# Zeros products for TensorE in the first tile of an RWKV-6 + GELU-MLP kernel: 24 instead of 8 in front, and four 64x64 products instead of two 128x128 ones behind each burst

## The chip, the cores and the metric

The kernel runs on one core of one Trainium2 chip. The metric is the device time of one execution in microseconds. All numbers are microseconds unless marked otherwise.

## What is computed

```python
# r, k, v, w: (4, 8, 768, 48); u: (8, 48)
for t in range(S):
    cur = einsum('bhd,bhe->bhde', u * k[t], v[t])
    y[t] = einsum('bhd,bhde->bhe', r[t], state + cur)
    state = w[t] * state + k[t] (outer) v[t]
x = y as (3072, 384)
h = x @ w_in                     # (3072, 2048)
out = (0.5 * h * (1 + erf(h / sqrt(2)))) @ w_out   # (3072, 384)
```

## The kernel before

The 768 time steps of four batches are cut into eight tiles of T = 384 steps; a tile holds all eight heads, and is cut into chunks of C = 64. For each tile, `attention(x, unit)` makes y (transposed, `xT`) and `mlp(x)` makes the output rows. Attention inside a chunk goes over levels h = 1, 2, 4, 8, 16, 32: on each level PE multiplies the chunk's k against its r in bursts of small products (`products`, L452), an elementwise update on VectorE (L494, L505) folds the decay w into r and k in place, and a masked copy (L465, L516 on VectorE, L513 on ScalarE) takes the level's part of the burst out of PSUM into `a_sb`. A burst of a level needs the update of the level before, and an update needs the burst of its own level to be through.

The first tile (x = 0) is done as two units of two head pairs each, so that work starts when half of the data is there. The two units alternate: a burst of one, a burst of the other. Each burst of the first tile has 24 fp32 products of 64x64 on the four 64x64 quadrants of the array; the profile lists 48, as each is two passes. The quadrant is set by the partitions of the operands and of the output: `half = [slice(0, 64), slice(64, 128)]`, rows by `g`, columns by `p`; `g` also picks one of the two PSUM banks of a `pair`. There are three such pairs (`pd`), so a burst may also have to wait for a copy to empty a pair.

The first level has two bursts a unit, the level's own and a diagonal one (`diagonal`, with r*u from ScalarE, L401). After the levels come the transposes of k (`kt_ps`, L685), the products of k and v (`kv_ps`, L711), those of `a_sb` and v (`y_ps`, L752), the chain of states on VectorE (L731, L726), the products of r and the states (L797), and copies and three plus three small DMAs into `xT`. Then the first burst of tile 1 (again L452), six products of zeros (`warm`, L225) and the first product of the MLP (`h_ps`, L1059) follow on PE. From then on PE is given a mix of MLP products and small attention bursts of the next tile.

`keep_warm(n)` issues n bf16 products of zeros, 128x128 by 128x512, into a bank of the tag "mm" that nothing reads. It is called with 8 ahead of everything, with 2 behind the bursts of the first tile (12 times: all but the first burst of each unit's first level), and twice with 3 (other banks) before the MLP starts.

The order of the work on each engine is written out by hand: `PLAN[x]` is a string in which each letter takes one step of a stream ("." the first unit or the MLP, "s" the second unit or the tile's attention, "l" loads, "c" weight conversion), and each engine executes its instructions in that order. All loads are issued by SyncE's queue, some only after a small memset on VectorE (L163, L204) has set a buffer free. The first tile's loads are, in order, w of both units, then r and k of the first unit and r and k of the second (L150).

Of the kernel before, what the change touches and what calls it, by code (L numbers as in the profile page):

```python
# [10 lines left out]
F32 = mybir.dt.float32  # L11
# [21 lines left out]
BANK = 512  # L33
# [40 lines left out]
def kernel(  # L74
# [9 lines left out]
    nc = tc.nc  # L84
# [16 lines left out]
    ps = ctx.enter_context(tc.tile_pool(name="ps", bufs=1, space=PSUM))  # L101
# [4 lines left out]
    def pair(name):  # L106
        return pools["d"].tile([128, 2, BANK], F32, name=name, tag="d")
# [16 lines left out]
    half = [slice(0, 64), slice(64, 128)]  # L124
# [8 lines left out]
    bufs = [io.tile([128, 3 * NP * T], F32, name=f"rkw{i}", bufs=1) for i in range(2)]  # L133
# [78 lines left out]
    zeros = const.tile([128, BANK], BF16, name="zeros")  # L212
# [6 lines left out]
    def keep_warm(n, elsewhere=False):  # L219
        if elsewhere:  # L220
            t = pair("warm")[:, 0]
        else:
            t = ps.tile([128, BANK], F32, name="warm", tag="mm", bufs=2)
        for _ in range(n):
            nc.tensor.matmul(t, lhsT=zeros[:, 0:128], rhs=zeros, start=True, stop=True)  # L225

    keep_warm(8)


    masks = {h: const.tile([128, C // 2], U8, name=f"mask{h}") for h in LEVELS if h < 16}  # L230
# [122 lines left out]
    def attention(x, unit):  # L353
# [91 lines left out]
        def products(bs, right, width, rest=False):  # L445
            d = pair("d")
            n = 0
            for b in bs:
                for i in range(NI):
                    for g in range(2):  # L450
                        for p in range(2):
                            nc.tensor.matmul(d[half[p], g, n * width:(n + 1) * width],  # L452
                                             lhsT=kc[half[g], b, i, p], rhs=right(half[g], b, i, p),
                                             start=True, stop=True)
                    n += 1
            if x == 0 and not rest:
                keep_warm(2)
            return d[:, :, 0:n * width]

        def diagonal():  # L460
            return [products([b], lambda z, b, i, p: rucs[b][z, i, p], C) for b in range(np_)]
# [7 lines left out]
        def halves():  # L469

            for h in LEVELS:
                m = C // 2 // h
                if np_ < NPART:

                    d = products(range(np_), lambda z, b, i, p: rc[z, b, i, p], C, h == 1)
                    d = d.rearrange("p g (n m two j) -> p g n m two j", two=2, j=h, m=m)[:, :, :, :, 1, :]
                else:
                    right = rc.rearrange("p b i c (m two j) -> p b i c m two j", two=2, j=h)[:, :, :, :, :, 1, :]
                    d = products(range(np_), lambda z, b, i, p: right[z, b, i, p], C // 2)
                    d = d.rearrange("p g (n m j) -> p g n m j", j=h, m=m)  # L480
# [220 lines left out]
        def vs(b, i, g):  # L701
            o = ((parts[b] * NI + i) * 2 + g) * D
            return loaded[x][1][:, o:o + G]

        kvs = []
        for b in range(np_):
            kv_ps = pair("kv_ps")
            for i in range(NI):
                for p in range(2):
                    for g in range(2):  # L710
                        nc.tensor.matmul(kv_ps[half[g], p, i * D:(i + 1) * D], lhsT=k_t(b, i, p, g),  # L711
                                         rhs=vs(b, i, g)[half[p], 0:D], start=True, stop=True)
# [74 lines left out]
        for i in range(NI):  # L787
            for p in range(2):
                for b in range(np_):
                    q, c3 = divmod(i, N3)  # L790
                    for g in range(2):
                        c = 2 * c3 + (p + g) % 2
                        src, c0 = (st, c - 1) if c else (before, NC - 1)
                        if src is None:
# [3 lines left out]
                                         lhsT=src[half[g], o:o + G], rhs=rc[half[g], b, i, c % 2],  # L798
                                         start=False, stop=True, skip_group_check=True)
# [518 lines left out]
```

## Time and profile before

| | us |
|---|---|
| timed runs | 588.53, 588.55, 589.37 (median 588.55) |
| profiled execution, device time | 589.61 |
| its span, first to last instruction | 587.8 |
| PE busy / weight loads busy | 571.1 / 521.4 |
| VectorE / ScalarE / GpSimd busy | 425.5 / 291.2 / 58.6 |
| mean granted TensorE clock | 0.997 |
| front: first zeros product; eight of them | 2.29; 3.59 |
| first real product (L452) | 9.43 |
| first transpose (L685) | 31.97 |
| first product of the MLP (L1059) | 44.40 |

The profile is of one execution. A line of it names the engine, the line of the kernel, the operation and the tiles, output before input; the bracket behind tells how long the engine stood idle before and what ended that. "issue" means that the profile shows nothing that the engine waited for. PE's products overlap, and their ends are modelled, so starts are the safer numbers.

### The profile page before, as it was taken

The page shows a single profiled execution, that of the slowest core. Times are in us where ns is not written, and L with a number is a line of the kernel's source. Part 1 is how long each engine was busy: PE and PEld are TensorE (multiplying, and loading weights), DVE is VectorE, ACT ScalarE, POOL GpSimd, SP SyncE. Part 2 cuts the span into 40 slices and gives each one's busy share as a digit, 9 for nine tenths or more (in the row PEclk, how much of TensorE's full clock was granted, in tenths as well). Part 3 has the DMA queues.
Part 4 walks back from the last instruction along what each step waited for, and adds up shares of the span by engine and source line. Part 5 has one row for each costly group of instructions (what it writes and reads, how often), then busy time and mean ns, then how long its engine had stood idle before and what let it go on. Part 6 is the DMA issues. An engine that isn't in the chain of part 4 may idle for free. (4 is left out here: it accounts for less than half of the span.)

```text
span 587.8 us, 17656 instructions
## 1 busy us (share of the span) xinstructions
PE 571.1 (97%) x7602; PEld 521.4 (89%) x7616; DVE 425.5 (72%) x825; ACT 291.2 (50%) x668; POOL 58.6 (10%) x63
## 2 busy tenths in 40 slices
PE   5789999999999999999999999999999999999997
PEld 3576666799999999999999999999998999999997
DVE  5988968989758975777959986777759987420332
ACT  2368898446362567235462467245561467335400
POOL 3100000013000130012000130002100111003100
PEclk8999999999999999999999999999999999999999
DMA  6749742253032542354122632344224333114201
GB/s 230 221 135 352 265 168 78 79 142 52 5 89 64 157 58 41 90 142 93 26 55 79 151 70 44 86 139 74 27 41 119 86 42 42 29 45 55 28 13 35
DMA packets 62430, 55.09 MB, mean 94 GB/s; under 512 B 32400, under 2 KB 47504, under 8 KB 62352
## 3 DMA queue, kind: packets, MB, share of 16 engines
q1 hardware_dynamic: 50832, 45.62, 25.5%
q0 software_dynamic: 11424, 8.26, 10.8%
q8 instruction: 60, 0.98, 0.7%
q14 instruction: 18, 0.15, 0.1%
q10 hardware_dynamic: 96, 0.07, 0.1%
HBM read 36.24 MB, written 4.72 MB: 70 GB/s over the span
## 5 line engine op out<-in xcount | busy, mean ns | idle before, releaser
L929 PE MATMUL h_ps<-xT,w_in_sb 128*128 128x192 f32 x560 | 111.5, 330 | 0.6 <-DVE o_sb L1196 0.6
L980 POOL DMA_DIRECT2D g<-o_sb x42 | 50.6, 1229 | 478.2 <-ACT o_sb L965 468.9
L929 PEld LDWEIGHTS h_ps<-xT,w_in_sb 128*128 128x128 f32 x560 | 93.0, 190 | 4.7 <-ACT g L961 1.6
L929 PE MATMUL u_ps<-s,w_in_sb 128*128 128x192 f32 x224 | 41.2, 327 | 0.0
L1073 PE MATMUL o_ps<-w_out_sb,g 128*128 128x192 f32 x224 | 39.8, 326 | 0.0
L929 PEld LDWEIGHTS u_ps<-s,w_in_sb 128*128 128x128 f32 x224 | 37.1, 190 | 0.2
L1073 PEld LDWEIGHTS o_ps<-w_out_sb,g 128*128 128x128 f32 x224 | 37.0, 190 | 0.0
L604 ACT COPY a_sb<-d 32x256 f32<-32x256 f32 (+8 forms) x90 | 32.6, 362 | 4.9 <-PE d L588 3.4
L1059 PE MATMUL h_ps<-xT,w_in_sb 128*128 128x384 f32 x96 | 33.2, 494 | 0.0
L452 PEld LDWEIGHTS d<-rkw 64*64 64x64 f32 x1152 | 19.4, 138 | 14.7 <-issue 10.5
L1073 PE MATMUL o_ps<-w_out_sb,f 128*128 128x192 f32 x176 | 32.0, 331 | 0.0
L1073 PE MATMUL o_ps<-t,g 128*128 128x192 f32 x176 | 31.4, 330 | 0.0
L1073 PE MATMUL o_ps<-t,s 128*128 128x192 f32 x176 | 31.2, 328 | 0.0
L1073 PE MATMUL o_ps<-t,e 128*128 128x192 f32 x176 | 30.6, 326 | 0.5 <-issue 0.5
L621 DVE COPY_PREDICATED a_sb<-quarter,d 128x480 f32<-128x480 uint8 (+5 forms) x54 | 23.2, 439 | 10.5 <-PE d L588 9.3
L726 DVE SCALAR_TENSOR_TENSOR st<-st,tot_sb,kv_ps 128x48 f32<-128x48 f32 x160 | 28.9, 258 | 2.6 <-PE kv_ps L711 2.5
L1073 PE MATMUL o_ps<-w_out_sb,e 128*128 128x192 f32 x176 | 30.7, 328 | 0.0
L982 DVE TENSOR_TENSOR g<-g,o_sb 128x384 f32<-128x384 f32 x14 | 7.6, 549 | 31.2 <-ACT o_sb L965 31.1
L1073 PEld LDWEIGHTS o_ps<-t,e 128*128 128x128 f32 x176 | 28.9, 190 | 0.7 <-issue 0.7
L1073 PEld LDWEIGHTS o_ps<-t,g 128*128 128x128 f32 x176 | 28.6, 190 | 0.5
L1073 PEld LDWEIGHTS o_ps<-w_out_sb,f 128*128 128x128 f32 x176 | 28.5, 190 | 0.6
L1073 PEld LDWEIGHTS o_ps<-t,s 128*128 128x128 f32 x176 | 28.8, 190 | 0.2
(163 smaller groups left out, 1171.3 us busy)
## 6 DMA issues: line engine op xcount, KB each, us to landing
rkw<-in_rkw_dram SPq DMA_DIRECT2D x54, 256.0 KB, 3.6
g<-o_sb POOLq DMA_DIRECT2D x42, 192.0 KB, 3.6
raw<-in_w_out_dram SPq DMA_DIRECT2D x8, 768.0 KB, 6.2
v_in<-in_v_dram SPq DMA_DIRECT2D x8, 584.0 KB, 4.6
raw<-in_w_in_dram SPq DMA_DIRECT2D x5, 768.0 KB, 7.5
out_dram<-o_sb SPq DMA_DIRECT2D x20, 192.0 KB, 2.0
rkw<-kx SPq DMA_DIRECT2D x72, 48.0 KB, 2.0
rkw<-in_rkw_dram SPq DMA_DIRECT2D x6, 384.0 KB, 6.2
```

The costliest lines, as they stand in the source:

```text
L452: nc.tensor.matmul(d[half[p], g, n * width:(n + 1) * width], lhsT=kc[half[g], b, i, p], rhs=right(half[g], b, i, p), start=True, stop=True)
L604: nc.scalar.copy(out=at[z, g, first:behind, (a + 1) * h:], in_=d[z, :, :, to] if g == slice(None) else d[z, :, to])
L621: nc.vector.copy_predicated(out=an[:, :, :, :, (a + 1) * h:], mask=mask.to_broadcast(data.shape), data=data)
L726: nc.vector.scalar_tensor_tensor(out=stq[:, q, c], in0=stq[:, q, c - 1] if c else b4[:, q, NC - 1], scalar=totq[:, q, c:c + 1], in1=kvs[q ...
L929: nc.tensor.matmul(o, lhsT=lhsT, rhs=rhs, start=start, stop=True, skip_group_check=True)
L980: nc.gpsimd.dma_start(out=g, in_=z, accum_op=ALU.add)
L982: nc.vector.tensor_add(g, g, z)
L1059: nc.tensor.matmul(h_ps, lhsT=w_in_sb[:, f // FI, j, f % FI * 128:(f % FI + 1) * 128], rhs=xT[:, j, :], start=(j == 0), stop=(j == NJ - 1))
L1073: nc.tensor.matmul(o, lhsT=lhs(j), rhs=rhs(j), start=start and j == 0, stop=(j == HF - 1), skip_group_check=True)
```

## The change

The front gets 24 products of zeros in place of 8. Behind the bursts of the first tile, `keep_warm(2)` is replaced by `keep_warm_tiles()`: four bf16 products of zeros of 64 rows, 64 columns and 512 elements, one on each quadrant of the array, the two row halves into the two banks of the tag "mm". The six zeros products before the MLP stay as they are. PE's instruction stream gets 32 more instructions in front (16 weight loads and 16 products) and 8 in place of 4 at each of the 12 fillers.

```diff
         for _ in range(n):
             nc.tensor.matmul(t, lhsT=zeros[:, 0:128], rhs=zeros, start=True, stop=True)
 
-    keep_warm(8)
+    def keep_warm_tiles():
+
+        ts = [ps.tile([128, BANK], F32, name="warm", tag="mm", bufs=2) for _ in range(2)]
+        for p in range(2):
+            for g in range(2):
+                nc.tensor.matmul(ts[g][half[p]], lhsT=zeros[half[g], 0:64], rhs=zeros[half[g]], start=True, stop=True)
+
+    keep_warm(24)
...
             if x == 0 and not rest:
-                keep_warm(2)
+                keep_warm_tiles()
             return d[:, :, 0:n * width]
```

## The prediction

> **What bounds the kernel now.** I read the page first, then the first 45 us by themselves, because both edits lie there. The page gives the balance and where PE's program comes from:
>
> ```profile
> PE 571.1 (97%) x7602; PEld 521.4 (89%) x7616; DVE 425.5 (72%) x825; ACT 291.2 (50%) x668; POOL 58.6 (10%) x63
> ...
> PEclk8999999999999999999999999999999999999999
> ...
> q8 instruction: 60, 0.98, 0.7%
> ```
>
> PE is the bound of the run: the trace's records show no PE gap over 0.1 us between 40.04 and 190 us, and only five, 1.7 us together, from there to the end. So whatever brings the first L1059 product (44.40) forward reaches the end, if nothing later takes it back. Queue q8 brought 60 blocks (0.98 MB) for 7616 weight loads, 7602 products and some 150 waits: 256 PE instructions a block. That matters below.
>
> The windows show the clock at the start:
>
> ```profile
> 9.00:10.00 1.00, 0.57 (x21) 0.60 (x25) 0.00 (x0) 0.56 (x2) 0.00 (x0) 0.68 0.99 402
> 10.00:11.00 1.00, 1.00 (x50) 1.00 (x46) 0.00 (x0) 0.74 (x2) 0.00 (x0) 0.50 0.85 339
> 11.00:12.00 1.00, 1.00 (x48) 1.00 (x43) 0.56 (x1) 0.38 (x1) 0.00 (x0) 0.50 0.32 128
> 12.00:13.00 1.00, 0.67 (x13) 0.22 (x6) 0.67 (x5) 0.00 (x0) 0.00 (x0) 0.61 0.18 62
> ```
>
> Columns: stretch, length, busy time (and instructions) of PE, PEld, DVE, ACT, POOL, granted clock, DMA share, GB/s. The 0.68 and the 0.61 put the half clock from 9.36 to 12.78, 3.42 us. The record has the rise before at 5.94, again 3.41 earlier. The first two real bursts fall just into the half clock.
>
> The timeline shows what that costs, what a filler costs, and where PE stands still:
>
> ```profile
> 2.29 3.59 PE L225 MATMUL warm<-zeros 128*128 128x512 bf16 x8 [2.29 <-ACT zeros L217]
> ...
> 9.43 1.56 PE L452 MATMUL d<-rkw 64*64 64x64 f32 x48 [3.55 <-DMA rkw<-in_rkw_dram]
> ...
> 10.74 1.54 PE L452 MATMUL d<-kx,rkw 64*64 64x64 f32 x48
> ...
> 12.33 0.56 DVE L494 TENSOR_TENSOR rkw<-rkw 128x384 f32<-128x384 f32 x1 [0.66 <-PE d L452]
> ...
> 13.00 0.93 PE L452 MATMUL d<-rkw 64*64 64x64 f32 x48
> ...
> 21.09 0.33 PE L452 MATMUL d<-rkw 64*64 64x64 f32 x3 [1.42 <-issue]
> ...
> 26.69 0.93 PE L452 MATMUL d<-rkw 64*64 64x64 f32 x48
> ...
> 27.55 0.39 PE L225 MATMUL warm<-zeros 128*128 128x512 bf16 x1
> ...
> 28.09 0.93 PE L452 MATMUL d<-rkw 64*64 64x64 f32 x48
> ```
>
> A burst takes 1.56 at half and 0.93 at full clock. From 26.69 on bursts start 1.40 apart, back to back with fillers, and DVE's updates wait for them (0.44, 0.43, 0.84 in the timeline): there PE sets the pace. From 12.33 to 22.42 DVE does, without a pause.
>
> The stall of 1.42 before 21.09 waits for no semaphore. The waits of the first 46 us (engine, line, what ended it: us in all, times, longest) have two more of the kind:
>
> ```profile
> PE d L452 <- issue: 1.8, 2, 1.4
> PE kv_ps L711 <- issue: 1.0, 1, 1.0
> ```
>
> They end at 21.09, 25.60 (0.35) and 37.43 (0.96); one of 0.54 ends at 447.6. Counting PE's weight loads twice plus its waits, they stand at instructions 705, 961, 1729 and 12481: 1, 3 and 42 blocks of 256 apart. These are waits for program blocks. A block starts to come about 1.2 us after the one before was begun, takes 0.9 to 1.8, and PE goes on 1.25 to 1.5 after its end. From one block's begin to the next one's arrival: 4.9 (16.2 to 21.09, in full DMA traffic), 4.5, at most 3.6, 3.1, 3.2 and 4.0; mean 3.9.
>
> **The change, part by part.** Front: eight products step 0.427 (weight loads at 2.70, 3.12, 3.55). The six at 43.1 step 0.216 at full clock. With the rise at 5.94, eight and a half of the 24 run slow and the rest take 15 x 0.216 and a bit: the last is through at 9.28. The first real burst needs its k at 9.35 and starts at 9.40, so the front delays nothing. PE has then been busy all through the stretch 5.94 to 9.36, so I take the fall at 9.36 to be gone. The burst at 9.40 ends at 10.33, the diagonal one at 11.2 instead of 12.28, and DVE's second L494 starts at 11.27, not 12.33: **-1.06**. DVE is packed behind it, so this carries on to the L505 at 21.46. Should the front gain nothing there, its cost is bounded by its overrun (rival one).
>
> Fillers: today the filler starts 0.15 after the burst's last product where products inside a burst step 0.058 by fours, and the next burst starts 0.53 after the filler: two steps of 0.216 and 0.10 more. Four products of 512 columns on the four quadrants exist in no row. If they run together as the burst's fours do, they cost 0.06 + 0.22 and the next burst starts 0.43 earlier; in pairs, 0.21 earlier; in turn, 4 x 0.216, 0.22 later. The nearest row is the burst itself (same tiles, same two banks by g), so I take -0.43 for each. It counts only where PE sets the pace. Both "mm" banks are now taken per call, but only PE writes them until y_ps, so that costs nothing.
>
> By the dependencies alone (burst 0.93, 0.06 to DVE, update 0.96, 0.05 back; the copies behind), the chain becomes: L505 of h=4 at 20.4 and 21.3, h=16 bursts at 24.2 and 25.6, h=32 bursts at 27.0 and 27.9 instead of 29.48 and 30.88, and the last L494 on k at 28.8 instead of 31.88. From there to the last L797 burst (40.04) the order is unchanged, but for the kv_ps stall, which held DVE's L731 back by 0.57 and is gone: 36.4, and the first L1059 at 40.8: **-3.6**.
>
> Program blocks: the front adds 32 PE instructions and each of 12 fillers 4, 80 in all. A burst with filler is now about 105 instructions, and at 3.9 us for 256 that is 1.6 us, more than the 1.28 a burst that the chain above wants. So blocks bind. Their borders move earlier by 32 + 4 for each filler passed: 449 falls behind the second diagonal burst (13.9), 705 into the first h=4 burst, 961 into h=8, 1217 into h=16, 1473 into the last h=32, 1729 to the start of the second kv_ps, 1985 ahead of the last L797, 2241 near the end of tile one's first burst (41.53 today). Seven round trips from 13.9: with the six above (23.3) and 3.5, block 2241 comes at 40.7, and 0.15 + six zeros products (1.31) later the first L1059, at 42.2: **-2.2**. Blocks and dependencies alternate: if the last h=32 burst must wait for its block until 30.9, the updates behind it give -1.4; if until 29.4, -3.0. I take the middle of these two, **-2.3**, next to the -2.2. [...]
>
> Sum: the profiled execution took 589.61 (span 587.8 and 1.8 around it), so 587.3 on its scale. The timed runs are 588.53, 588.55 and 589.37. The 1.06 between profile and median may be the profiler's, or the half clock fell elsewhere in those runs and the front's -1.06 is partly had already. I split it: 588.55 - 1.85 = **586.7**; the ends -3.6 on the median and -1.4 on the profile's scale give 585.0 to 588.2.
>
> **Rivals.** (1) The clock rises later. Only this run's phase of the 3.41 us steps ends the front at 9.28. A rise at 9.1 gives 16 slow products and an end at 10.8: the first burst 1.4 late, DVE's L494 at 12.7, +0.35 against before, and fillers and blocks still give about -1.2: 587.7. For it: 589.37 beside 588.5 shows runs that differ by about this. Against: front and rise lay well here. [...] Chance 0.17.
>
> (2) Slower: program blocks become the bound outright. 13.9 + 7 round trips + 1.46 reaches 44.40 at 4.15 us a trip; 3.9 was the mean before. At 4.4, because denser PE work asks for blocks while the loads of tile one (14.28 to 22) fill the DMA engines, the first L1059 comes 1.8 late: 590.3. For it: 4.9 and 4.5 in just that traffic. Against: four of six were 4.0 or less. Chance 0.2, half of it near 588.5.
>
> (3) The clock falls back, as the lighter fillers leave PE less busy. The least busy 3.41 us that kept the full clock was 19.6 to 23.0, PE busy 1.85 (54%), by its records. My chain has 0.93 + 0.22 in about 1.4 to 1.75, 65% or more; a block stall of 1.5 in one window goes under 54%. Two falls make some five bursts 0.63 longer, +3.1: 589.8. Chance 0.08.
>
> (4) The four tiles run in turn: the change does not do what it says, +0.22 a burst where PE sets the pace, which eats the -1.06: 588.5. Chance 0.05.
>
> **How the numbers follow.** The forecast has 0.5. About 0.2% (1.2 us) is what a measurement of this kernel can tell from no change. Faster by more means under 587.4: most of the forecast's own range and part of (1): 0.58. Slower, above 589.7: half of (2), most of (3), and a late front in (1) with slow blocks: 0.19. The rest, 0.23, lies between. The range 585.0 to 589.2 leaves out the upper half of (2) and (3).
>
> **What would show it.** Right: clock 1.00 from 9 to 13; 48 products of the first burst in 0.93; L494 at about 11.3; bursts with filler about 1.0 apart where they aren't held; gaps "issue" ahead of PE at instructions 256 apart, in the last h=32 burst or the second kv_ps; first L1059 at 41.5 to 43. Wrong: front still running at 10; a granted clock of 0.50 after 13; 64x512 products 0.2 apart; issue stalls beyond 4 us in sum; or an L1059 two us earlier whose gain is gone by the end.

## The result and the profile after

The changed kernel is slower. Six executions took 590.44 to 594.81 us, median 592.67, beside a median of 588.98 for six of the kernel before: ratio 1.0061, 95% interval 1.0040 to 1.0083. A second comparison gave 591.75 against 588.36, ratio 1.0043 (1.0022 to 1.0065). The forecast was 586.7, with 585.0 to 589.2 as its range.

The profiled execution took 590.44 (span 588.7), against 589.61 (587.8) before: +0.83. So the two profiles show only a part of the slowdown: the profiled execution of the changed kernel was the fastest of its six, and that of the kernel before was slower than all six timed beside it. The other executions come below.

The windows of the start (stretch, length, busy time of PE, PEld, DVE, ACT, POOL, granted clock, DMA share, GB/s) show that the front did what it was counted on for:

```profile
9.00:10.00 1.00, 1.00 (x36) 0.55 (x37) 0.00 (x0) 0.61 (x2) 0.00 (x0) 1.00 1.03 419
10.00:11.00 1.00, 1.00 (x80) 1.00 (x71) 0.47 (x1) 0.69 (x2) 0.00 (x0) 1.00 0.87 343
11.00:12.00 1.00, 0.95 (x52) 0.66 (x45) 0.92 (x6) 0.43 (x1) 0.00 (x0) 1.00 0.26 101
12.00:13.00 1.00, 0.48 (x32) 0.37 (x25) 0.96 (x2) 0.00 (x0) 0.00 (x0) 1.00 0.29 66
```

The clock is 1.00 where it was 0.50, and the first two bursts take 0.93 and 0.91 instead of 1.56 and 1.54. The timeline of PE then shows where that goes:

```profile
2.29 7.19 PE L225 MATMUL warm<-zeros 128*128 128x512 bf16 x24 [2.29 <-ACT zeros L217]
9.48 0.93 PE L459 MATMUL d<-rkw 64*64 64x64 f32 x48
...
15.30 0.40 PE L232 MATMUL warm<-zeros 64*64 64x512 bf16 x2 [1.34 <-issue]
...
20.13 0.62 PE L459 MATMUL d<-rkw 64*64 64x64 f32 x25 [1.98 <-issue]
20.53 0.39 PE L232 MATMUL warm<-zeros 64*64 64x512 bf16 x3
...
20.75 0.91 PE L459 MATMUL d<-rkw 64*64 64x64 f32 x47
...
24.13 0.27 PE L459 MATMUL d<-rkw 64*64 64x64 f32 x1 [1.35 <-issue]
...
27.58 0.63 PE L459 MATMUL d<-rkw 64*64 64x64 f32 x27 [0.19 <-issue]
...
31.47 0.28 PE L459 MATMUL d<-rkw 64*64 64x64 f32 x4 [1.21 <-issue]
...
36.59 0.80 PE L718 MATMUL kv_ps<-v_in,kx 64*64 64x48 f32 x40 [0.87 <-issue]
...
40.59 1.32 PE L804 MATMUL y_ps<-rkw,st 64*64 64x64 f32 x38 [1.33 <-DVE fence L769]
...
44.05 0.32 PE L459 MATMUL d<-rkw 64*64 64x32 f32 x9 [0.82 <-issue]
...
45.61 4.03 PE L1066 MATMUL h_ps<-xT,w_in_sb 128*128 128x384 f32 x12
```

Seven gaps end in "issue". They and the one at 40.59 stand at PE instructions 449, 705, 961, 1217, 1473, 1729, 1985 and 2241, every border of 256 in turn. The gap at 40.59 is put down to a fence on VectorE, but that fence was done at 39.71; the program block of that border ended its transfer at 39.16, and PE went on 1.43 later, as it did 1.2 to 1.5 after the block at every other border. The "issue" gaps before the first product of the MLP sum to 7.8 us; before the change those at borders summed to 2.7. That product (L1066, formerly L1059) starts at 45.61, not 44.40: +1.21, of which 0.8 is left in the span. The times of block transfers here and below are those of queue q8's packets in the trace.

### The profile page after: what moved, and what is told of

It is laid out like the page before. It is cut to its first block, busy times and chain, and to the rows that moved or that the text cites. A ratio compares the mean times of both kernels' runs of the same rounds, so it can differ in the third digit from the quotient of the medians.

```text
span 588.7 us, 17745 instructions
## 1 busy us (share of the span) xinstructions
PE 571.9 (97%) x7654; PEld 521.9 (89%) x7656; DVE 424.8 (72%) x825; ACT 291.2 (49%) x668; POOL 58.6 (10%) x63
## 5 line engine op out<-in xcount | busy, mean ns | idle before, releaser
L1066 PE MATMUL h_ps<-xT,w_in_sb 128*128 128x384 f32 x96 | 33.2, 494 | 0.0
L1080 PE MATMUL o_ps<-w_out_sb,e 128*128 128x192 f32 x176 | 30.7, 328 | 0.0
L1080 PEld LDWEIGHTS o_ps<-w_out_sb,e 128*128 128x128 f32 x176 | 28.7, 190 | 0.2
```

Of the source, the lines that this page charges most:

```text
L1066: nc.tensor.matmul(h_ps, lhsT=w_in_sb[:, f // FI, j, f % FI * 128:(f % FI + 1) * 128], rhs=xT[:, j, :], start=(j == 0), stop=(j == NJ - 1))
L1080: nc.tensor.matmul(o, lhsT=lhs(j), rhs=rhs(j), start=start and j == 0, stop=(j == HF - 1), skip_group_check=True)
```

## Experiments

**The same kernel again, and the clock by execution.** No edit.

> The changed kernel a second time, for a second trace. Theory one (program blocks): PE again stands still at every border of 256 instructions from the front to the first product of the MLP; that product comes at 45 to 46.5 us, a block trip takes 3.4 to 5 us. Theory two (granted clock): in most executions the clock falls back to half for one 3.41 us step or more somewhere between 13 and 45 us, because a block stall leaves PE idle too long; each such step costs about 2 us. Both together: 591 to 594 us. If only theory one held, the time would be 590.5 in every execution.

Measured: 591.75 (590.16 to 593.15), ratio 1.0043. In its trace PE again stood still at seven of the eight borders, and the first L1066 came at 46.22. At border 449 only the weight loads paused, while products still ran, and PE went on at 13.97, not at 15.30; border 2241 came later than in the first trace:

```profile
13.97 0.11 PEld L232 LDWEIGHTS <-zeros 64*64 64x64 bf16 x2 [0.18 <-issue]
...
44.66 0.32 PE L459 MATMUL d<-rkw 64*64 64x32 f32 x9 [1.64 <-issue]
```

After its first rise the clock held throughout that trace. Each execution also has its mean granted clock, and one half-clock step of 3.41 us takes 0.003 off it (0.997 in the profile of before, which has one). Time ahead of the first recorded rise counts as full clock (that profile's view has 1.00 from 0 to 5 us, where the front's products start 0.427 apart). Put together, the 16 executions of the changed kernel in both comparisons and the 31 of the kernel before in this one:

| mean granted clock | before | changed |
|---|---|---|
| 1.000 | 588.7 (12) | 590.6 (4) |
| 0.997 | 588.5 (14) | 592.5 (9) |
| 0.994 or less | 591.1 (2) | 592.8 (3) |

(mean us, executions in brackets; three of before at 0.996 and 0.999 are left out.) In the profile of before, the half-clock step falls where the front has gone idle (PE busy 0.00 in the 3.42 us ahead of it). What it costs can't be read from the column of before, as an execution at 1.000 may have had a late first rise instead (tiles_only, below). In the changed kernel the front held the clock in both traces, so a 0.997 should mean one step later on; such executions took 1.9 longer. The other 1.9 is there even where the clock never fell after its rise. So the change costs about 1.9 without a fall (the blocks, less what front and fillers gain), and a fall about 1.9 more. This split is an estimate: it rests on four executions at 1.000, and a second step (0.994 or less) added only 0.3.

**The parts alone.** The first kernel has 24 products in front and the old fillers, the second 8 in front and the new fillers.

```diff
-    keep_warm(8)                 # front_only
+    keep_warm(24)
...
-                keep_warm(2)     # tiles_only
+                keep_warm_tiles()
```

> 24 products in front, fillers as before (two of 128x512). Adds 32 of the 80 PE instructions, so the first product of the MLP stays ahead of the eighth block border. Theory one (blocks): six trips instead of seven lie before the last L797 burst, which starts at 39.9 to 40.7 us as before; total 588 to 589.5, within 0.2% of before, so the 1.06 us won at the first bursts is lost again to blocks. Theory two (clock): the heavy fillers keep the full clock, so no half clock after 13 us and no run above 590. Rival (the front costs by itself, running late when the clock rises late): 590 or more.

> 8 products in front, fillers on four 64x64 tiles. Adds 48 of the 80 PE instructions; the first product of the MLP comes to lie just behind the eighth block border. Theory one (blocks): first product of the MLP at 44.5 to 46 us, total 589 to 590.5. Theory two (clock): light fillers and stalls let the clock fall in some executions beyond the step at 9.4 us, total 590 to 593. Rival (the fillers alone, without blocks and clock, as in the forecast): 587 or less.

Measured: front_only 588.65, ratio 0.9994 (0.9972 to 1.0016), nine of ten executions at clock 1.000. tiles_only 590.35, ratio 1.0023 (1.0001 to 1.0045), eight of ten at 0.997. The full clock of the first bursts, bought with 32 instructions, is thus worth nothing that can be measured. The new fillers alone do harm, just clear of noise; what the front adds to it isn't clear of noise, as the intervals of tiles_only and of the changed kernel's second comparison (1.0022 to 1.0065) overlap. In the trace of tiles_only the clock first rose only at 14.64, so its first bursts were slow; later the trace caught a fall of the clock:

```profile
31.71:35.12 3.41, 2.97 (x123) 2.65 (x127) 2.96 (x11) 2.81 (x5) 0.00 (x0) 1.00 0.85 265
35.12:38.53 3.41, 0.74 (x50) 0.62 (x44) 1.27 (x9) 2.37 (x3) 0.00 (x0) 1.00 0.46 156
38.53:41.95 3.42, 3.42 (x105) 3.42 (x98) 2.23 (x13) 0.00 (x0) 0.00 (x0) 0.50 0.02 5
```

```profile
12.03 1.53 PE L459 MATMUL d<-rkw 64*64 64x64 f32 x48
...
38.03 0.56 PE L718 MATMUL kv_ps<-v_in,kx 64*64 64x48 f32 x24 [2.67 <-issue]
```

A border stopped PE for 2.67 us inside kv_ps. In the 3.41 us that hold this stall PE was busy for 0.74 (22%), and the next 3.41 us, in which y_ps and the L804 bursts run, are at 0.50. So this fall is put down to the block stall. No trace of the changed kernel caught one; that its falls have the same cause is inferred.

**The instruction count alone.** PE's work stays as before, in more and shorter full-size products: as many instructions as in the changed kernel, no small tile.

```diff
-    keep_warm(8)
+    pieces_of_zeros(24, 171)         # 24 products of 171 columns
...
-                keep_warm(2)
+                pieces_of_zeros(4, BANK // 2)   # 4 of 256 columns
```

> The PE work of the kernel before, cut into as many instructions as the changed kernel has: the front is 24 products of 171 columns instead of 8 of 512, each filler 4 full-size products of 256 columns instead of 2 of 512; no product on small tiles. Theory one (program blocks): PE stands still at the same borders as in the changed kernel, the first product of the MLP comes at 45 to 46.5 us, and the time is 590 to 592, +0.3% to +0.6% on the kernel before. Rival (the small tiles, or the lighter or later zeros products themselves, make the change slower): as before, within 0.15%.

Measured: 591.22 (589.55 to 597.15), ratio 1.0040 (1.0007 to 1.0072), as much as the changed kernel lost in its second comparison (1.0043), with no more zeros to multiply than before (4104 columns in front for 4096). One execution took 597.15; the medians alone differ by 0.24%. In its trace a filler still delays the next burst by 0.54 (from 24.67 to 25.21), where the old one took 0.53. Its first product of the MLP came at 46.36, behind stalls at five of the same borders, four of them shown:

```profile
24.41 0.33 PE L457 MATMUL d<-rkw 64*64 64x64 f32 x3 [1.38 <-issue]
...
36.98 0.84 PE L716 MATMUL kv_ps<-v_in,kx 64*64 64x48 f32 x42 [0.69 <-issue]
...
40.98 1.33 PE L802 MATMUL y_ps<-rkw,st 64*64 64x64 f32 x40 [1.33 <-issue]
...
44.71 0.41 PE L457 MATMUL d<-rkw 64*64 64x32 f32 x10 [1.01 <-issue]
```

This settles the main cause: 80 more PE instructions ahead of the MLP are enough for a loss, without more PE work and without small tiles. How much of the changed kernel's loss they make, the interval leaves wide.

**Fewer instructions.** One filler product instead of two, then none; the front stays at 8.

```diff
-                keep_warm(2)
+                keep_warm(1)      # one_filler; no_filler drops the call
```

> 8 products in front, one filler product of 128x512 instead of two behind each burst: 24 PE instructions fewer than before, 104 fewer than the changed kernel, and half of the filler's PE time. Theory one (blocks): fewer instructions, so less waiting; if the clock holds, first product of the MLP 0.5 to 1.5 us earlier than 44.4, total 587.3 to 588.5. Theory two (clock): half the filler lets the clock fall back in some executions, 2 us each: 589 to 592. The granted clock of each run tells which.

> 8 products in front, no filler behind the bursts of the first tile: 48 PE instructions fewer than before, 128 fewer than the changed kernel. Theory one: one_filler with 24 fewer took 586.7 on average where the clock did not fall back and the kernel before 588.6, so here 585 to 586.5 in such executions. Theory two (clock): without fillers the clock falls back in most executions, 2 to 3 us each: 588 to 590 in these. If fillers mattered for the clock alone and blocks for nothing, every execution would be slower than before.

Measured: one_filler 588.37, ratio 0.9986 (0.9957 to 1.0015). Its six executions at 0.996 and above took 585.2 to 590.1, mean 587.2, its four at 0.994 took 589.8 on average; the trace of one of the latter has a stall of 2.73 in y_ps, ending at 36.77, and a half-clock step from 36.19 on. no_filler 587.81, ratio 0.9976 (0.9947 to 1.0006). Only one of its ten executions came into the 585 to 586.5 that I expected, and none was at 1.000; its three executions at 0.994 took 587.5 on average, the three at 0.990 and 0.991 589.3. In its trace the first product of the MLP came at 42.36, 2 us earlier than before, with the half clock only from 9.58 to 12.99. No gain from the fillers can be measured.

**The front's time in half of its instructions.** Six fp32 products of 512 columns are 12 passes, 24 instructions (the trace of long_front lists 12 products for the six); then the same with fewer filler instructions.

```diff
-    keep_warm(8)
+    keep_warm_long(6)            # long_front: fp32 zeros, 128x128 by 128x512
...
-                keep_warm(2)
+                keep_warm(1)     # lean; long_front_bare drops the call
```

> The front's PE time of the changed kernel in half of its instructions: 6 fp32 products of zeros with 512 columns (12 passes, 24 instructions, where 24 bf16 products are 48 and the 8 of before 16); fillers as before. Only 8 instructions more than before, and the clock up before the first real burst. If the first bursts at full clock are worth something once blocks do not take it back: 587 to 588, 0.1% to 0.3% faster than before. If the block that comes at about 12.9 us and the trips behind it set the pace whatever the clock does: 588 to 589, as before and as front_only.

> The front of long_front (6 fp32 products) and one filler product of 128x512 instead of two: 16 PE instructions fewer than before. Both theories together: blocks cost less than before (as in one_filler, 586.7 where the clock stays up), and the clock still falls back in part of the executions, as light fillers and a stall near 35 us leave PE idle. Expected 586 to 588 at the median, the best of all kernels so far if the front's full clock adds to one_filler.

> lean a second time, for a closer interval: 6 fp32 products in front, one filler product of 128x512; 16 PE instructions fewer than before. Theory one: faster by 0.2% to 0.4%, first product of the MLP at about 42.4 us again.

> 6 fp32 products in front, no fillers: 40 PE instructions fewer than before, 24 fewer than lean. If instructions alone decide: 585 to 586.5, a little faster than lean. If the clock falls back more often without any fillers, as it did in no_filler (6 of 10 executions under 0.997): as lean or up to 1.5 us slower, 587 to 588.5.

Measured: long_front 0.9996 (0.9972 to 1.0020), as front_only. lean 586.99, ratio 0.9968 (0.9942 to 0.9994), again 587.30, ratio 0.9976 (0.9953 to 0.9999). long_front_bare 587.31, ratio 0.9974 (0.9952 to 0.9995), no better than lean though it has 24 instructions fewer: ten of its twelve executions had a half-clock step or more (0.997 and less), lean in its two comparisons nine of 22. The waits of lean's first 46 us have 3.5 us of "issue":

```profile
PE d L459 <- issue: 2.4, 5, 0.7
...
PE y_ps L759 <- issue: 1.1, 1, 1.1
```

That is more than the 2.7 before: with less PE work between them, the borders are reached sooner and waited at. Still its first L1066 starts at 42.38 and 41.96 in the two traces, where the kernel before had 44.40. But lean also has half of the fillers' zeros, so its gain is not shown to come from the 16 instructions. And single traces differ: front_only, with 32 instructions more than before, had its first L1059 at 42.98 in its fastest execution (586.85).

**The small tiles at an equal instruction count.** Each filler is two products on two opposite tiles instead of two full-size ones; then the long front with a single product on one tile.

```diff
-                keep_warm(2)
+                keep_warm_tiles()     # two_tiles: for g: ts[g][half[g]] only
```

> 8 products in front, each filler two products of 64x512 on two opposite 64x64 tiles: exactly as many PE instructions as before, and a shorter filler. This tells the forecast's filler term (next burst 0.43 us earlier, where PE sets the pace) apart from the blocks. If the shorter filler were worth something by itself: 586.5 to 587.5, faster by 0.2% or more. Theory one (blocks set the pace of the first 45 us, so time saved between two borders is waited out at the next): as before within 0.15%. In the trace bursts with filler about 1.0 us apart where no border lies between.

> The two ideas of the change with fewer PE instructions than before: the front as 6 fp32 products (24 instructions), each filler a single product of 64x512 on one 64x64 tile (2 instructions instead of 4): 16 PE instructions fewer than before, 96 fewer than the changed kernel. Blocks, and the shorter filler that two_tiles showed to be worth 0.3%: 585.5 to 587, faster by 0.3% to 0.6%, first product of the MLP at 41.5 to 42.5 us. If the light filler lets the clock fall back in most executions: 587 to 588.5.

Measured: two_tiles 587.07, ratio 0.9970 (0.9949 to 0.9992), with its three executions at 1.000 at 585.88 to 586.05. That is against my theory: I had expected a shorter filler to be waited out at the next border, and it is so only in part (3.3 us of "issue" in its trace, the first L1065 at 42.28). So in the kernel before, the blocks alone don't set the pace of the first 45 us. long_front_tile 588.32, ratio 0.9974 (0.9952 to 0.9996); that the two ideas add is not seen. Its trace has stalls of 1.67 ending at 20.79 and 2.62 ending at 37.37 and a half-clock step at each, and its four executions at 0.994 or less took 589.8 on average.

Four versions beat the kernel before by 0.2% to 0.3% (lean, two_tiles, long_front_bare, long_front_tile), and so the changed kernel by 0.7% to 0.9% by the quotients of the ratios. Their intervals overlap; which of them is best stays open.

## Why the prediction was wrong

**Clock at the start: right, and worth nothing that was measured.** The front ended at 9.28 by the sum; the first real burst came at 9.48, at full clock, and VectorE's L501 on r ran at 10.53, the one on k right behind it, as laid out. In the changed kernel VectorE kept the lead as far as its second L512 (17.44, before 18.64). Then the stalls took it: the last L494 on k, here L501, came at 31.87 (before 31.88). The trace of front_only, with just this part, kept the lead as far as there:

```profile
30.80 0.56 DVE L494 TENSOR_TENSOR rkw<-rkw,tot_sb 128x384 f32<-128x384 f32 x1 [0.84 <-PE d L452]
```

That was the fastest of ten executions, though, and the ten together have a ratio of 0.9994. Why the lead doesn't show there stays open.

**Filler price: right.** Behind the stall at 20.13 a filler starts at 20.53 and the next burst at 20.75, 0.22 later, where the old filler took 0.53. The forecast's own terms (0.15 and 0.53 against 0.06 and 0.22) give 0.40, not 0.43. Four tiles do run at once (the four products at 10.90 take 0.42 together, the one at 16.08 takes 0.38); rival four is out. two_tiles shows that a shorter filler is worth something as long as it brings no instructions (ratio 0.9970).

**Program blocks: the right mechanism, mis-sized; this is the step that failed.** The chain of blocks was put at 13.9 for border 449 and seven trips to border 2241 at 40.7. The first trace has 15.30 and 44.05, the second 13.97 and 44.66. So the start of the chain came as forecast in the second. It was 1.4 late in the first, where border 193 was passed at 10.48 and the block of border 449 started to come only at 12.95; in the second trace border 193 was passed at 10.63 and that block started at 11.64. What failed in both is the seven trips: they took 28.75 and 30.7, or 4.1 and 4.4 each, where 3.83 was counted (23.3 for six and 3.5). The part of a trip that came out longer is the one between a border and the start of the next transfer. It was put at about 1.2; over the seven trips it was 1.1 to 3.1, on average 1.8 and 1.9. The transfers took 0.9 to 1.5, and PE went on 1.2 to 1.6 after their end, much as counted. The profile of before had a 2.6 already (border 449 passed at 16.14, transfer from 18.77 on). In the first trace +1.4 and +1.95 make +3.35, and -2.2 + 3.35 is about the +1.2 by which the first L1066 moved; in the second +0.1 and +3.9 make +4.0, and the first L1066 moved by +1.8. Twice a trip took about 5 us (15.30 to 20.13, and 31.47 to 36.59, where the transfer began 3 us after the border). Why some transfers begin that late was not tried; the DMA engines were between 52% and 93% busy in these stretches, which shows nothing either way.

The weighing failed, too. Rival two had this very chain and a limit of 4.15 a trip; with 3.9 as the mean before, it deserved more than 0.2. The forecast took -2.3 as the middle of -1.4 and -3.0, which is -2.2. With -2.2 by the blocks alone and -3.6 by the dependencies alone, a chain that has to keep to both can't come out better than -2.2.

**Clock falls: seen, and given too little.** Rival three named a block stall that leaves PE idle in one step, and put it at 0.08. By the mean clock it happened in 12 of 16 executions, which took 1.9 to 2.2 longer than the others; it had about 1.55 a fall (3.1 for two).

**Late rise of the clock (rival one).** The first rise came at 5.94 before, 6.05 and 6.49 in the two traces of the changed kernel, and at 5.30 in long_front, so the phase moves; in tiles_only, with the old front, it came only at 14.64. At 6.49 the front ended late enough to put the first burst at 9.63, 0.15 later than at 6.05. In the two traces of the changed kernel this decided nothing.

**The scale.** Half of the 1.06 between the profiled execution and the first three timed ones was taken off. The kernel before, executed 31 times beside the second copy, ranged from 585.91 to 592.54; three runs could not carry such a term, nor a "0.2% can be told from no change".

## What to carry to other kernels

Where a stretch consists of very short products, count PE's instructions, not only its time. Here a block of 256 took about 4.1 us to come, which makes an estimate of 16 ns for each instruction where the blocks bind, also where it adds no PE work, as in padded. The 80 of padded cost 2.4 us (interval 0.4 to 4.2); the 32 of front_only cost nothing that was measured. Look for gaps that wait for no semaphore, see whether they lie 256 instructions apart, and if they do, judge every added filler by its instructions too: shorter fillers in as many instructions, or half of the zeros in fewer, gained 0.2% to 0.3%, where the small tiles with 80 more instructions lost 0.4% to 0.6%. And when two limits alternate, the later one is the best case. Read a trace together with the other executions: one alone can be the fastest or the slowest of its kernel.

## What the runs showed of the hardware that was not expected

The time from PE passing a border to the start of the next transfer was anything from 0.3 us (tiles_only, 11.22 to 11.47) to 3.8 us (tiles_only, 31.91 to 35.72). Passing the border sooner didn't always bring the block sooner: with the border at 193 passed at 11.64 (before), 10.48 and 10.63 (changed), the transfer of the next block started at 12.90, 12.95 and 11.64.

A stall of 2.67 us on a block was followed by 3.41 us at a granted clock of 0.50 (tiles_only). In the traces, stretches of 3.41 us that lost the full clock after the first real burst had PE busy for 22% to 37% (0.74 us in tiles_only; 1.25 from 32.78 to 36.19 in one_filler); 49% kept it (1.67 us from 16.62 to 20.04 in two_tiles). Not every such stretch is a block's work: in long_front_bare the one from 16.95 to 20.36 (1.24 us, 36%) holds waits of 0.92 and 1.05 for VectorE.
